# Nystrom attention and a multiplicative feed-forward on one core: transposes moved to VectorE, a recalibrated planner with searched due times, and the 32x32 iteration of two batches in one step

## The chip, the cores and the metric

The kernel runs on one core of one Trainium2 chip. The metric is the device time of one execution, in microseconds; the median of three runs is given. The engines are TensorE (PE), VectorE (DVE), ScalarE (ACT), GpSimd (POOL) and SyncE (SP, which only issues transfers). Each has its own queue and works through it in order; engines meet at semaphores.

## The reference

For each of 8 batches and 8 heads (576 rows, 64 columns), in cut form:

```python
q_lm = q.reshape(B, H, 32, 18, D).mean(axis=3)      # landmarks: means over 18 rows
k_lm = k.reshape(B, H, 32, 18, D).mean(axis=3)
A  = softmax(scale * q    @ k_lm.T)                 # 576 x 32
Bm = softmax(scale * q_lm @ k_lm.T)                 # 32 x 32
C  = softmax(scale * q_lm @ k.T)                    # 32 x 576
Z  = Bm.T / (norm1(Bm) * norminf(Bm) + 1e-6)
for _ in range(6):
    Z = 2 * Z - Z @ Bm @ Z
x = heads_side_by_side(A @ Z @ C @ v)               # 4608 x 512
out = ((x @ w1) * (x @ w2) @ w3) @ w_out            # 4608 x 512
```

## The kernel before

The work is cut into quads, a quad n being four heads of one batch (16 quads, n = 2b + qd), and into batches b (8).

For a quad, two POOL transfers load k and q as fp16 into `nat` (L387). A transposing transfer on SP turns both into `T` (`trans`, L417). POOL sums 18 rows to one (`mean_a`, `mean_b`, L424 to L436), scales the means into `lm` (`mean_c`, L438), and a second transposing transfer on SP makes `lmT` (`lm_trans`, L450). PE computes the scores of C and B into a PSUM pair of their own, `psS` (`s_mm`, L457), and the scores of A (`a_mm`, L533). DVE takes maxima, ACT exponentials, DVE the 32x32 block transposes `ecT` and `aT` (L529, L589); POOL normalises A into `ah` (L582).

For a batch, PE multiplies C with v (`cv_mm`, L640; v is loaded with zeros beside it, so that two heads share 128 rows), DVE and ACT do B's softmax (`b_soft_a` to `b_soft_c`, L669 to L693), and the iteration runs as one PE step and one DVE step five times (`it_mm` L726, `it_out` L736), then Z (L748, L758), W = (Z C v) transposed (L768, L776), and U = W w1 and W w2, 4 x 16 matmuls of 512 columns (L784), which ACT copies to `u` (L798).

The dense part d1 multiplies `u` with `aT`: for a chunk of 288 rows and each of 8 blocks j, four matmuls of 288 columns fill two PSUM banks, one for w1 and one for w2 (`d1_mm`, L854); ACT copies the first out (`d1_a`, L864) and DVE multiplies it with the second into `ab` (`d1_b`, L869). d2 (`d2_mm`, L876) multiplies `ab` with `w34` = w3 @ w_out, eight matmuls of 512 columns for 128 rows; ACT scales it into `osb` and SP stores it in four transfers (L883, L889). `w34` is made in the kernel: `w3` comes in fp32, PE transposes it, ACT and DVE split it into a high and a remaining fp16 part, and 192 matmuls of 512 columns follow (L290 to L350).

The order on all engines is written by a planner (`Plan`, L39). Each piece of work is a task with an engine, an assumed duration, the tasks it needs, slots that it takes from rings of buffers, slots that it frees and a priority. `run` (L86) simulates the engines: at each step it starts the task that can begin first, among near ones that of lowest priority value, and the list that results is the program's order. Priorities are due times: batch b's dense part is due at 66 + 25.5 b (L232 to L243). PSUM is a ring "P" of six banks for everything but `psS`. `wof`, the landing place of w_out, lies in `vbs`, and `ab` is laid over the memory of w34's inputs, so every d1 task waits for the last w34 task (`deps + ["wo7"]`, L908).

Of the kernel before, what the change touches and what calls it, by code (L numbers as in the profile page):

```python
# [20 lines left out]
NC9 = 9  # L21
DM = 512
DF = 1024
HALF = 288
# [3 lines left out]
LOW = -1e30  # L28


class Task:
    def __init__(self, name, eng, dur, fn, deps, acq, rel, prio, mode, lat, move, after):
        self.name, self.eng, self.dur, self.fn = name, eng, dur, fn
        self.deps, self.acq, self.rel = deps, acq, rel
        self.prio, self.mode, self.lat, self.move, self.after = prio, mode, lat, move, after
        self.start = self.ready = None


class Plan:  # L39
# [3 lines left out]
    LAT = {"PE": 0.25, "ACT": 0.08, "DVE": 0.08, "POOL": 0.1, "SP": 0.0}  # L43
    SWITCH = 0.1
# [8 lines left out]
    def add(self, name, eng, dur, fn, deps=(), acq=(), rel=(), prio=0.0, mode=None, lat=None,  # L53
            move=0.0, after=0.0):
        t = Task(name, eng, dur, fn, list(deps), list(acq), list(rel), prio, mode,
                 self.LAT[eng] if lat is None else lat, move, after)
        self.by[name] = t
        self.tasks.append(t)
        return t

    def _slots(self, acq):

        got, when, taken = [], 0.0, {}
        for ring, key, n, uses in acq:
            free = self.rings[ring]
            used = taken.setdefault(ring, set())
            if n == 1:
# [3 lines left out]
                best = min(some, key=lambda i: (free[i], -(free[i ^ 1] is None) if ring == "P" else 0, i))  # L71
                pick = [best]
            else:
# [5 lines left out]
                best = min(some, key=lambda i: max(free[i], free[i + 1]))  # L79
# [5 lines left out]

    def run(self):  # L86
        free = {e: 0.0 for e in self.LAT}
        mode, moved = None, 0.0
        todo = list(self.tasks)
        waiting = {t.name: sum(1 for d in t.deps) for t in todo}  # L90
        after = {}
        for t in todo:
# [3 lines left out]
        for t in todo:  # L96
            if not waiting[t.name]:
                t.ready = 0.0
                avail[t.eng].append(t)
        order = []  # L100
        n = len(todo)
        while len(order) < n:
            best = None
            for e, cand in avail.items():
                opts = []
                for t in cand:
                    found = self._slots(t.acq)
                    if found is None:
                        continue
                    at = max(free[e], t.ready, found[0], t.after)  # L110
                    opts.append((at, t, found[1]))
                if not opts:
                    continue
                first = min(o[0] for o in opts)
                near = [o for o in opts if o[0] <= first + (0.05 if e == "PE" else 0.0)]
                at, t, got = min(near, key=lambda o: (
                    o[1].prio - (0.6 if e == "PE" and o[1].mode == mode else 0.0)))
                if best is None or at < best[0]:
                    best = (at, t, got)
            if best is None:  # L120
                left = [t.name for t in todo if t.start is None]
# [5 lines left out]
            dur = t.dur  # L127
            if e == "PE":
                if t.mode != mode:
                    dur += self.SWITCH  # L130
                mode = t.mode
            free[e] = at + dur
            end = at + dur + t.lat
            if t.move:
                moved = max(moved, at + dur) + t.move
                end = moved + t.lat
            t.end = end
# [5 lines left out]
            for key in t.rel:  # L143
                rec = self.left[key]
                rec[0] -= 1
                rec[1] = max(rec[1], end)
# [3 lines left out]
            for u in after.get(t.name, ()):  # L150
                waiting[u.name] -= 1
                if not waiting[u.name]:
                    u.ready = max(self.by[d].end for d in u.deps)
                    avail[u.eng].append(u)
            order.append(t)
        return order


@with_exitstack
def kernel(  # L160
# [18 lines left out]
    psS = banks[3]  # L179
# [8 lines left out]
    P.ring("P", 6)  # L188
    P.ring("S", 1)
    nats = slots(fixed, 4, [128, 2, GRP, D], FP16, "nat")  # L190
    Ts = slots(fixed, 3, [128, 2 * NC9, 128], FP16, "T")
    lsum = slots(fixed, 1, [128, 2, NC9, D], FP32, "ls")
    lm16 = slots(fixed, 2, [128, 3, 2, D], FP16, "lm")
# [801 lines left out]
```

## Time and profile before

| what | us |
|---|---|
| median of three runs | 351.21 |
| the three runs | 348.2, 351.21, 351.9 |
| span of the profiled execution (first instruction to last) | 343.6 |
| PE busy by records | 277.7 |
| DVE, ACT, POOL busy by records | 201.0, 148.4, 154.2 |

The profiled execution is listed by its span alone; no time of its own beside it is given. A record of a PE instruction ends where the profiler models its result to be complete, so records of neighbours overlap, and the busy time of an engine is the union of its records. In the groups, the figures are busy time and the mean of one instruction, then the idle time of the engine ahead of them and who ended it.

### The profile page before, as it was taken

The numbers are of one execution on the slowest core, as the hardware profiler recorded it, in microseconds if no ns is written. First come the engines' busy times: TensorE is split into PE (matmuls) and PEld (weight loads), VectorE is DVE, ScalarE is ACT, GpSimd is POOL, SyncE is SP. The second block draws the span as 40 slices with busy tenths as digits, with TensorE's granted clock in tenths as the row PEclk, the third lists the DMA queues.
The fourth block names the chain that finished last, engine by engine and source line by source line (L and its number), as shares of the span: only waits on it lengthen the run. The fifth ranks groups of instructions, "written<-read, shape, count | busy, mean of one in ns | idle before, by whom it ended". The sixth has DMA issues, their size and how long they took to land.

```text
span 343.6 us, 10423 instructions
## 1 busy us (share of the span) xinstructions
PE 277.7 (81%) x4288; PEld 152.7 (44%) x4288; DVE 201.0 (58%) x499; ACT 148.4 (43%) x349; POOL 154.2 (45%) x197
## 2 busy tenths in 40 slices
PE   3689888987738878897978899889898887997972
PEld 2244444633523534454535554544455444544531
DVE  7623546461987855684887487755867773432420
ACT  3522332405432344364526555653655255436432
POOL 6498594399783662655485583637011010000000
PEclk9999999999978969999999999999999999999998
DMA  8987989998897886369887997776541210221223
GB/s 214 358 184 152 220 223 207 178 195 177 133 220 82 144 187 129 73 128 192 180 161 169 188 190 144 173 156 138 126 108 32 56 39 3 60 65 32 60 62 93
DMA packets 64175, 48.39 MB, mean 141 GB/s; under 512 B 48256, under 2 KB 48256, under 8 KB 64128
## 3 DMA queue, kind: packets, MB, share of 16 engines
q1 hardware_dynamic: 58368, 36.19, 47.1%
q0 software_dynamic: 5760, 11.54, 20.8%
q8 instruction: 33, 0.54, 0.7%
q14 instruction: 14, 0.11, 0.1%
HBM read 38.80 MB, written 9.44 MB: 140 GB/s over the span
## 4 chain that ended last, share of the span: by engine, by line
PE 44%; DVE 19%; ACT 13%; DMA 11%; issue 5%; SPq 3%; POOL 3%; ACTq 0%; DVEq 0%; POOLq 0%
PE bank L228 44%; DVE ab L872 5%; ACT asb L866 4%; DMA nat<-in_q_dram 4%; ACT u L800 4%; DMA lmT<-lm 3%; DMA vb<-in_moe_w_out_dram 3%; ACT osb L885 2%; DMA vb<-in_v_dram 2%; POOL ls L427 1%; DVE xz L739 1%; DVE xz L722 1%; DVE bm L673 1%; ACT ec L513 1%; SPq L293 1%
## 5 line engine op out<-in xcount | busy, mean ns | idle before, releaser
L228 PE MATMUL bank<-aT,u 128*128 128x288 f16 x512 | 84.0, 291 | 17.2 <-DVE ab L872 8.0
L872 DVE TENSOR_TENSOR ab<-asb,bank 128x288 f16<-128x288 f16 x128 | 55.9, 447 | 56.5 <-ACT asb L866 31.9
L866 ACT CAST asb<-bank 128x288 f16<-128x288 f32 x128 | 49.9, 404 | 72.6 <-PE bank L228 59.9
L228 PE MATMUL bank<-w,ab 128*128 128x512 f16 x288 | 73.7, 382 | 3.5 <-ACT osb L885 1.2
L228 PEld LDWEIGHTS <-u 128*128 128x128 f16 x512 | 47.1, 98 | 48.4 <-issue 28.4
L228 PE MATMUL bank<-wo,w3t 128*128 128x512 f16 x192 | 48.9, 387 | 6.5 <-DVE w3t L331 3.8
L434 POOL TENSOR_TENSOR ls<-ls 128x512 f32<-128x512 f32 (+1 forms) x64 | 46.6, 728 | 4.5
L427 POOL TENSOR_TENSOR ls<-nat 128x1152 f32<-128x1152 f16 x16 | 37.8, 2366 | 20.6 <-DMA nat<-in_q_dram 20.0
L800 ACT CAST u<-bank 128x512 f16<-128x512 f32 x64 | 35.2, 598 | 19.1 <-PE bank L228 12.2
L228 PEld LDWEIGHTS <-ab 128*128 128x128 f16 x288 | 26.9, 98 | 29.0 <-issue 7.0
L885 ACT ACTIVATE osb<-bank 128x512 f32<-128x512 f32 x36 | 21.5, 598 | 30.3 <-PE bank L228 17.1
L582 POOL TENSOR_TENSOR ah<-ea,tiny 128x576 f16<-128x576 f32 x16 | 18.5, 1158 | 29.0 <-DVE tiny L577 21.2
L521 POOL TENSOR_TENSOR tiny<-tiny,maskS 128x4 f32<-128x4 f32 x16 | 3.2, 201 | 61.3 <-ACT ec L513 61.3
L228 PEld LDWEIGHTS <-w3t 128*128 128x128 f16 x192 | 17.8, 98 | 26.9 <-issue 9.7
L228 PE MATMUL bank<-xz 32*32 32x64 f32 (+1 forms) x768 | 20.5, 223 | 11.3 <-DVE xz L722 4.6
L228 PE MATMUL bank<-w,wT 64*32 64x512 f16 x512 | 22.8, 388 | 7.8 <-ACT u L800 2.2
L331 DVE SCALAR_TENSOR_TENSOR w3t<-bank,w3t 128x512 f16<-128x512 f32 x16 | 10.9, 685 | 27.1 <-ACT w3t L324 19.4
L228 PEld LDWEIGHTS bank<-xz 32*32 32x32 f32 x768 | 13.0, 108 | 28.2 <-issue 12.3
L739 DVE SCALAR_TENSOR_TENSOR xz<-xz,bank 128x128 f32<-128x128 f32 x40 | 11.4, 284 | 16.8 <-PE bank L228 16.0
L513 ACT ACTIVATE ec<-bank,tiny 128x320 f32<-128x320 f32 x32 | 16.8, 529 | 9.2 <-DVE tiny L506 8.9
L348 ACT ACTIVATE w<-bank 128x512 f16<-128x512 f32 x8 | 4.8, 596 | 35.0 <-PE bank L228 35.0
L228 PE MATMUL bank<-vb,ecT 128*32 128x128 f32 x576 | 18.0, 273 | 0.1
(75 smaller groups left out, 320.0 us busy)
## 6 DMA issues: line engine op xcount, KB each, us to landing
vb<-in_v_dram SPq DMA_DIRECT2D x64, 144.0 KB, 4.1
out_dram<-osb SPq DMA_DIRECT2D x144, 64.0 KB, 1.7
nat<-in_k_dram POOLq DMA_DIRECT2D x16, 288.0 KB, 5.3
nat<-in_q_dram POOLq DMA_DIRECT2D x16, 288.0 KB, 7.0
w3n<-in_moe_w_dram SPq DMA_DIRECT2D x8, 512.0 KB, 6.9
vb<-in_moe_w_out_dram SPq DMA_DIRECT2D x8, 256.0 KB, 8.6
w<-in_moe_w_dram POOLq DMA_DIRECT2D x8, 256.0 KB, 8.7
T<-nat SPq DMA_TRANSPOSE x16, 5.9
```

What stands on the lines that cost most here:

```text
L228: nc.tensor.matmul(out_, lhsT, rhs, start=start, stop=stop, **({} if pos is None else {"tile_position": pos}))
L331: nc.vector.scalar_tensor_tensor(out=t[:, 1, 512 * h:512 * h + 512], in0=bank(at(f"ptr{j}{h}")), scalar=WSC, in1=t[:, 0, 512 * h:512 * h + ...
L348: nc.scalar.activation(out=w34[:, j, :], in_=bank(at(f"pw{j}")), func=AXF.Copy, scale=1.0 / (WSC * WSC))
L427: nc.gpsimd.tensor_tensor(out=l, in0=nat[:, :, 0:9, :], in1=nat[:, :, 9:18, :], op=ALU.add)
L434: nc.gpsimd.tensor_tensor(out=l[:, :, x:x + m, :], in0=l[:, :, x:x + m, :], in1=l[:, :, y:y + m, :], op=ALU.add)
L513: nc.scalar.activation(out=ecs[at(f"ec{n}")][:, hp, :, :], in_=psS[:, :, 160 * hp:160 * hp + 160], func=AXF.Exp, scale=SCALE, bias=t[:, 2 ...
L582: nc.gpsimd.tensor_tensor(out=ahs[at(f"ah{n}")], in0=eas[at(f"ea{n}")], in1=tinies[at(f"ta{n}")][:, 0:18].unsqueeze(2).to_broadcast([128, ...
L739: nc.vector.scalar_tensor_tensor(out=new.rearrange("p s t x -> p (s t x)"), in0=xz.rearrange("p s t x -> p (s t x)"), scalar=2.0, in1=bank ...
L800: nc.scalar.copy(out=uu[at(f"u{b}{qd}")][:, wi, 512 * half:512 * half + 512], in_=bank(at(f"pU{b}{wi}{half}{qd}")))
L866: nc.scalar.copy(out=asb[at(f"as{b}{j}{ch}")], in_=bank(at(f"pD{b}{j}{ch}0"))[:, 0:HALF])
L872: nc.vector.tensor_mul(abs_[at(f"ab{b // 2}")][:, j, c0:c0 + HALF], asb[at(f"as{b}{j}{ch}")], bank(at(f"pD{b}{j}{ch}1"))[:, 0:HALF])
L885: nc.scalar.activation(out=osb[at(f"os{g}{t}")], in_=bank(at(f"pE{g}{t}")), func=AXF.Copy, scale=2.0 ** -12)
```

## The change

What stays the same: the operations of d2, U, W, w34's 192 matmuls, the split into high and remaining parts, POOL's sums. What changes:

- q, k, the landmarks and `aT` are transposed on DVE as pairs of fp16, taken as one fp32: `T`, `lmT` and `ah` hold pairs side by side, and the scores run as two accumulating matmuls over 32 rows each (e = 0, 1) in place of one over 64. The transposing transfers on SP are gone. B's scores are a nineteenth group of A's, so B's softmax is part of A's; `b_norm` (DVE) writes it to `bm`.
- The scaling of the means moves from POOL to ACT. The swap of maxima is one matmul. v is loaded without zeros, and C runs as 64-row by 32-column tiles.
- w3 is loaded in four transfers of 1 KB rows for each block, transposed on DVE in 32x32 blocks instead of on PE, and w_out lies in `u` and `ab`. `ab` has memory of its own, in four pieces of 384 rows, so d1 doesn't wait for `wo7`; only d2 does.
- The iteration runs for groups of batches: `GROUPS` of one, two, two, two and one.
- d1 has chunks of 192 rows: w1's and w2's part lie in one bank. PSUM is one ring of eight banks; the scores take pairs from it.
- A store is two transfers of 64 partitions instead of four of 32.
- The planner has other costs and latencies, models the two DMA queues, and its due times are two tables, `ANCHOR` (one for each w3 block, quad, batch, dense chunk and group) and `OFF` (one for each kind of task).

The diff, cut to its core:

```diff
-HALF = 288
+CH = 192
+GROUPS = ((0,), (1, 2), (3, 4), (5, 6), (7,))
...
-    LAT = {"PE": 0.25, "ACT": 0.08, "DVE": 0.08, "POOL": 0.1, "SP": 0.0}
-    SWITCH = 0.1
+    LAT = {"PE": 0.23, "ACT": 0.16, "DVE": 0.13, "POOL": 0.1, "SP": 0.0}
+    SELF = {"PE": 0.0, "ACT": 0.14, "DVE": 0.11, "POOL": 0.05, "SP": 0.0}
+    SWITCH = 0.093
+    FIRST, LAND = 1.4, 0.6
...
+ANCHOR = {
+    "z": 0.0, "w0": -55.6, "w1": -74.9, "w2": -57.5, "w3": -88.7, "w4": -90.5, "w5": -59.7, "w6": -54.2,
...
+    "d7": 134.6, "d8": 173.8, "d9": 24.5, "d10": 25.8, "d11": 32.3, "d12": -83.6, "d13": 5.2, "d14": 95.8,
...
-    P.ring("P", 6)
-    P.ring("S", 1)
+    P.ring("P", 8)
...
     def w3_tr(j, h):
-                nc.tensor.transpose(out=ps[:, 128 * i:128 * i + 128],
-                                    in_=w3n[at(f"w3n{j}")][:, 128 * c:128 * c + 128],
-                                    identity=ident[:, :])
+            nc.vector.transpose(
+                out=w3f[at(f"w3f{j}")][:, 4 * h:4 * h + 4].rearrange("p e g i -> p (e g i)"),
+                in_=w3n[at(f"w3n{j}")][:, :, 128 * h:128 * h + 128]
+                .rearrange("p g (e x) -> p e g x", x=32))
...
-    def trans(n):
-            nc.sync.dma_start_transpose(
-                out=Ts[at(f"T{n}")][:, :, :],
-                in_=nats[at(f"nat{n}")].rearrange("p t r d -> p (t r d)"))
+    def trans(n, t):
+            nc.vector.transpose(
+                out=Ts[at(f"T{n}")][:, t].rearrange("p r l e -> p (r l e)").bitcast(FP32),
+                in_=nats[at(f"nat{n}")][:, t].rearrange("p r d -> p (r d)").bitcast(FP32))
...
     def mean_c(n):
+            nc.scalar.activation(out=lm16[at(f"lm{n}")], in_=lsum[at(f"ls{n}")][:, :, 0, :],
+                                 func=AXF.Copy, scale=1.0 / GRP)
...
     def lm_trans(n):
+            nc.vector.transpose(
+                out=lmTs[at(f"lmT{n}")].rearrange("p t l e -> p (t l e)").bitcast(FP32),
+                in_=lm16[at(f"lm{n}")].rearrange("p t d -> p (t d)").bitcast(FP32))
...
     def s_mm(n):
+            for e in range(2):
+                for hh in range(4):
...
+                        mm(ps[o:o + 32, hp, 0:288], lm[r, 1, :, e],
+                           T[r, 0, 9 * t:9 * t + 9, :, e].rearrange("p r l -> p (r l)"),
+                           start=(e == 0), stop=(e == 1), pos=(32 * hh, o))
...
     def a_mm(n):
+            for g in range(GRP + 1):
+                for e in range(2):
+                    for hh in range(4):
+                        r = slice(32 * hh, 32 * hh + 32)
+                        w = lm[r, 1, :, e] if g == GRP else T[r, 1, g, :, e]
+                        mm(ps[r, g, :], w, lm[r, 0, :, e], start=(e == 0), stop=(e == 1),
+                           pos=(32 * hh, 32 * hh))
...
     def a_norm(n):
+                out=ahs[at(f"ah{n}")].rearrange("p g m e -> p g e m"),
...
+    def b_norm(n):
+            nc.vector.tensor_tensor(
+                out=bms[at(f"bm{i}")][:, 0, n - 2 * GROUPS[i][0], :], in0=eas[at(f"ea{n}")][:, GRP, :],
+                in1=tinies[at(f"ta{n}")][:, GRP:GRP + 1].to_broadcast([128, M]), op=ALU.mult)
...
     def cv_mm(b):
+                        mm(ps[o:o + 32, qd, 0:D], ecTs[at(f"ecT{n}")][r, hp, c, :],
+                           vbs[at(f"vb{n}")][r, hp, c, :], start=(c == 0), stop=(c == 8),
+                           pos=(r.start, o))
...
-    def it_mm(b, i):
-            for s in range(2):
+    def it_mm(i, x):
+            for s in range(2 * len(GROUPS[i])):
...
+    def d1_ps(b, j, ch):
+        return bank(at(f"pD{b}{j}{ch}"))[:, 0:2 * CH].rearrange("p (w x) -> p w x", w=2)
...
     def d2_store(i):
+            for x in range(2):
...
+                    in_=o_sb[64 * x:64 * x + 64, :])
...
-                acq = [("P", f"pD{b}{j}{ch}{wi}", 1, 1) for wi in range(2)]
-                add(f"d{b}{j}{ch}", "PE", 0.5, d1_mm(b, j, ch), deps=deps + ["wo7"], acq=acq,
+                add(f"d{b}{j}{ch}", "PE", 0.33, d1_mm(b, j, ch), deps=deps,
+                    acq=[("P", f"pD{b}{j}{ch}", 1, 1)],
```

More of the change, by code (lines that the diff above doesn't have):

```diff
@@ L151, in run @@
                 waiting[u.name] -= 1
+                same = t.eng == u.eng and not t.dma
+                u.ready = max(u.ready, t.free + self.SELF[e] if same else t.end)
                 if not waiting[u.name]:
-                    u.ready = max(self.by[d].end for d in u.deps)
                     avail[u.eng].append(u)
@@ new lines, in quad_tasks @@
+        add(f"lv{n}", "SP", 1.9, load_v(n), acq=[("vb", f"vb{n}", 1, 1)],
+            at=(l, -9.0 + qd), early=-3.0, floor=12.0, dma=("SP", 2.0),
+            kind="lv")
+        loads = [f"lq{n}0", f"lq{n}1"]
+        for t in range(2):
+            add(f"T{n}{t}", "DVE", dve(576), trans(n, t), deps=[loads[t]] + ([f"T{n}0"] if t else []),
+                acq=[] if t else [("T", f"T{n}", 1, 2)], rel=[f"nat{n}"], at=(p, -6.0 + t), kind="T")
+        add(f"ma{n}", "POOL", 2.4, mean_a(n), deps=loads, acq=[("ls", f"ls{n}", 1, 1)],
+            rel=[f"nat{n}"], at=(p, -8.0), kind="mean")
```

806 lines of the change are left out of this document (370 added, 436 removed), and 12 rows, old and new, of tables (ANCHOR, OFF).

## The prediction

> **What bounds the kernel now.** I read the page's busy shares and slices first, then the engine waits of the tensor engine (PE), then the groups by shape, the timeline for the true pace of a matmul, and the DMA queue's waits.
>
> ```profile
> span 343.6 us, 10423 instructions
> PE 277.7 (81%) x4288; PEld 152.7 (44%) x4288; DVE 201.0 (58%) x499; ACT 148.4 (43%) x349; POOL 154.2 (45%) x197
> ...
> PE   3689888987738878897978899889898887997972
> ...
> PE 44%; DVE 19%; ACT 13%; DMA 11%; issue 5%; SPq 3%; POOL 3%; ACTq 0%; DVEq 0%; POOLq 0%
> ```
>
> PE looks full, but less than half of the chain that ends last is PE. The waits of PE say who holds it:
>
> ```profile
> PE bank L228 <- DVE ab L872: 12.6, 23, 1.6
> ...
> PE bank L228 <- ACT u L800: 5.1, 12, 1.0
> PE bank L228 <- DVE xz L722: 4.6, 2, 3.3
> PE bank L228 <- ACT asb L866: 4.5, 15, 0.7
> PE bank L228 <- DVE w3t L331: 3.8, 6, 1.0
> PE bank L228 <- ACT osb L885: 3.5, 7, 0.9
> ```
>
> The first column is us in total. Four of these (L872, L800, L866, L885; 25.7 us) are waits for a PSUM bank to be emptied. The timeline gives the pace behind the records:
>
> ```profile
> 320.81 1.14 PE L228 MATMUL bank<-aT,u 128*128 128x288 f16 x8
> ...
> 326.15 0.65 PE L228 MATMUL bank<-aT,u 128*128 128x288 f16 x4
> ...
> 327.96 1.03 PE L228 MATMUL bank<-w,ab 128*128 128x512 f16 x4
> ...
> 332.22 4.04 PE L228 MATMUL bank<-w,ab 128*128 128x512 f16 x18 [0.69 <-ACT osb L885]
> ```
>
> Four more 288-column matmuls take 1.14 - 0.65 = 0.49 us, 122.5 ns each; fourteen more of 512 take 3.01 us, 215 ns each: 224 more columns in 92.5 ns are 2.4 columns per ns, with 2.5 ns beside them. A record lasts 286 or 379 ns, so a stretch that ends in a wait carries a tail of 0.16 us.
>
> PE's work, at these paces and, for the small kinds, from the start of one group in the timeline to that of the next: d1 512 x 0.1225 = 62.7; d2 288 x 0.215 = 61.9; W3*W_out 192 x 0.215 = 41.3; U 32 x 0.43 = 13.8 (sixteen of 512 columns, eight side by side); C 8 x 2.08 (66.91 to 68.99) = 16.6; the iteration 8 x (0.27 + 5 x 0.36 + 0.26) = 18.6 (72.10 to 72.46); scores 16 x (S 0.28, A 0.32, swap 0.17) = 12.3 (from 46.50 and 63.26); w3 transposes 16 x 0.44 (45.32 to 45.76) = 7.0; W 8 x 0.38 = 3. Together 237 us, 69% of the span. The other 106: idle 343.6 - 277.7 = 66; a clock of 0.84 and 0.83 in 100 to 140 us, 40 x 0.165 = 6.6; the rest, some 33, tails. So the kernel is bound by waits of PE, in a fixed order, and the work itself is a floor far below.
>
> **The change, part by part, on PE.** The w3 transposes leave PE: -7.0. C was 72 passes of 128 columns, four tiles side by side; it becomes 144 of 64 columns, eight side by side, so half of 2.08: -8.3. A was 40 matmuls of 64 columns in 0.32 us and becomes 152 of 32, four side by side: by columns 1.9 times, 0.61 us, by count 3.8 times, 1.22; the row is the same kind of stream of small tiles, so I take columns: 16 x 0.29 = +4.6 (end +14.4). S's sixteen matmuls double in columns (0.15 to 0.30, from the starts at 46.50 and 46.65) and lose four for B: +0.3. The swap becomes one matmul: -1.5. The iteration runs in five groups instead of eight; of a step's 0.36 us, columns are 16 x 64 x 2 / 4 / 2.4 = 0.21, so merging two batches saves a restart of 0.15 in each of 7 steps, three times: -3.2. d1 is 768 matmuls of 192 columns, 80 + 2.5 ns each, 63.4: +0.7. d2, U and w34 stay. Sum -14.4, to 223.
>
> The weights of d1 bear a second look. A weight load's record is 98 ns, longer than the 82.5 ns of the new matmul; if it could not be hidden, 768 x 15.5 = +12 us. At 288 columns the pace is columns alone, which shows it hidden there; I take zero and keep 12. [...]
>
> **The waits.** d1 held two of six banks and now holds one of eight, so three times as many can be under way while ScalarE (ACT) and VectorE (DVE) empty them. Of the 25.7 us I let a third stay: -17. What is late next is DVE's multiply itself. The iteration's waits (L722, L739, L719, L760, L743, L689, L664, L712, L780, L489, L687: 16.8 us) fall with five chains for eight: -6. Both ends are 0 and all of it. The waits for w3 halves (L331 and L324, 5.6) and its second load go by half: -3; the first load at 4.76 us stays. The lmT transfer on PE: -1.4. Tails go with the stops, 33 to 18: -15 (ends 0 and -25). Both dips of the clock come just after PE's thinnest stretch (6.3 of 10 us busy in 90 to 100); a denser PE should not have them: -6.6 (end 0).
>
> **The other engines.** DVE gains, by rows: q/k transposes 32 x 0.77 (L529's 0.835 at 640, less 64 columns at 0.96 per ns) = 24.6; landmark transposes 16 x 0.245 (L691) = 3.9; w3 transposes 16 x 0.70 = 11.2; d1 products 192 x 0.347 against 55.9, +10.7; B's normalisation 16 x 0.225 = 3.6. It loses B's softmax and copy, 16.4, half of aT's transposes, 4.8, and some 10 in iteration, maxima and constants. Net +23 on records that sum to 222. Two L872 back to back take 0.82 for 2 x 0.45, so 0.08 of each record overlaps: occupied 182 now, 201 after (some 548 instructions). In 287 us that is 70%, hidden beside PE's 78% as long as the order alternates. ACT: 192 x 0.32 for 49.9, +11.7, and the mean's scaling +5: 148 to 163, hidden. GpSimd (POOL): loses 16.8 (mean's scaling), 8.5 (memsets), 3.2 and four issues; its normalisation now writes every second fp16: between its row 1.16 and the 2.37 of L427, up to 16 x 1.2 = 19 on an engine at 43%; I take zero.
>
> SP loses 32 DMA transposes and half of the 144 stores, and gains 24 w3 issues at about 0.45 us, 11 us, in the first stage, where v's loads wait behind them; hidden, since before it needed the time for transposes:
>
> ```profile
> SPq L419 <- PE bank L228: 30.9, 12, 4.3
> SPq L419 <- DMA nat<-in_q_dram: 23.7, 6, 17.1
> SPq L452 <- POOL lm L445: 19.2, 5, 7.3
> ```
>
> These waits do not vanish: the transposes that stood in SP's queue now stand in DVE's, with the d1 products and the iteration behind them, and PE's banks behind those. If the order places them late enough they cost nothing, which I assume.
>
> DVE operations with two SBUF inputs vary while others do not: L722 has a mean of 683 ns and 213 at best, L673 618 and 224, L743 440 and 224, L689 426 and 225, mean excess 320; L739, with one input in PSUM, keeps 284.
>
> ```profile
> L722 DVE TENSOR_TENSOR xz<-bm,tiny 128x64 f32<-128x64 f32 x8 | 5.5, 683 | 0.0
> L739 DVE SCALAR_TENSOR_TENSOR xz<-xz,bank 128x128 f32<-128x128 f32 x40 | 11.4, 284 | 16.8 <-PE bank L228 16.0
> L529 DVE STREAM_TRANSPOSE ecT<-ec 128x640 f32<-128x640 f32 x16 | 13.4, 835 | 1.6 <-ACT ec L513 1.4
> ```
>
> The change adds 32 such (16 w3 remainders, whose source was PSUM; 16 of B) and removes 22: 10 x 0.32 = 3 us of DVE, hidden. [...]
>
> **Sum.** 343.6 - 14.4 - 17 - 6 - 3 - 1.4 - 15 - 6.6 = 280.2. The profiled execution has no time of its own beside its span; the median of 351.2 lies 7.6 above it, and I add that: 287.8, say 287.
>
> **Rivals.** (a) More than that: all bank and iteration waits go and tails fall by 25: 280.2 - 8.7 - 10.8 - 10 = 250.7, so 258 at best, about 268 in the middle. For it: banks are eight, and PE's records already fill 9.69 of the 10 us from 20 to 30; against: DVE at 75 to 80%. (b) DVE becomes the bound: 201 + 13 (42 two-input operations by 0.32), at the 69% that PE gets now from a fixed order, 310, with 7.6 it is 318. For it: DVE is 19% of the chain already. (c) Only the work goes, and the waits move to new places: 343.6 - 14.4 + 7.6 = 337. (d) Weight loads and the small matmuls of A cost their upper ends, 12 + 9.8: 309. [...] (e) Slower: DVE waits in order for loads, as SP did. All of 30.9 + 23.7 + 19.2 = 74 us put on DVE and PE: 287 + 74 = 361. It decides from 64 us on, 1.3 us for each of the 48 moved transposes. For it: a place in a fixed queue cannot move when a load is late; against: L419's 30.9 are waits for a free buffer, and DMA without 48256 small packets should land earlier than now (q 7.0 us).
>
> **Chances.** Forecast (274 to 302) 0.44; (a) 0.16; (b) 0.13; (c) 0.08; (d) 0.05; (e) 0.12; no change 0.02. Faster by over 1% is 0.86, within 1% 0.02 (about what a measurement here can tell), slower 0.12. The range must leave out 0.2: (e) and no change, and 0.06 of the ends of (a) and (c): 262 to 338.
>
> **What would show it.** Right: records of d1 at 192 columns with starts 82 ns apart; A near 0.6 us; PE's waits on L872's successor below 9 us; a clock of 1.00 after the first 15 us; q/k transposes near 0.77 us with no wait for a DMA ahead of them. Wrong: DVE over 80% busy with PE waiting on it, transposes that wait for loads, or PE starts of d1 98 ns or more apart. The forecast falls if the searched order leaves PE's idle time near 66 us.

## The result and the profile after

| | before | after |
|---|---|---|
| median of four runs, same chip | 351.55 us | 440.12 us |
| ratio, 95% interval | 1 | 1.2508 (1.2391 to 1.2624) |
| span of the profiled execution | 343.6 us | 433.7 us (its time: 435.43) |
| granted TensorE clock, mean | 0.978 | 0.869 |
| PE busy; idle (span less busy) | 277.7; 65.9 | 295.0; 138.7 |
| pairs of weight load and matmul on PE | 4288 | 6728 |

A pair is one weight load and the matmul that follows it: two instructions of PE. Some executions of each kernel are slower than its others; ratios leave these out, and the profiled executions of the runs b1 and s4 below are such ones, so that of them only the place and kind of the waits is relied on.

The change costs 88.6 us where 64 were forecast to be gained. The page of the changed kernel, in the parts shown of before:

```profile
span 433.7 us, 15201 instructions
PE 295.0 (68%) x6728; PEld 188.8 (44%) x6728; DVE 218.3 (50%) x540; ACT 157.6 (36%) x421; POOL 124.8 (29%) x137
...
PEclk9999999986559975579879886579979998999999
...
q8 instruction: 52, 0.85, 0.8%
```

No engine is fuller than it was: DVE is at 50%. The clock row has three holes. The last line (packets, MB) is the queue that brings instructions; before, it had 33 packets:

```profile
q8 instruction: 33, 0.54, 0.7%
```

At 128 pairs to a packet (worked out below), 52 packets are 6656 of PE's 6728 pairs, and 33 are 4224 of 4288: the queue carries PE's instructions. The waits of PE (us in total, times, longest) name two things ahead of all others:

```profile
PE bank L277 <- issue: 57.5, 28, 5.5
PE bank L277 <- ACT w3t L349: 40.4, 1, 40.4
PE bank L277 <- DVE ab L860: 10.0, 18, 1.6
PE bank L277 <- ACT u L781: 9.0, 16, 1.4
PE bank L277 <- ACT asb L854: 6.5, 16, 0.8
PE bank L277 <- ACT osb L874: 2.7, 5, 0.7
```

Before, the same two stood at:

```profile
PE bank L317 <- DMA w3n<-in_moe_w_dram: 6.8, 2, 4.8
...
PE bank L228 <- issue: 0.3, 1, 0.3
```

`issue` is time in which PE waited for nothing that the profile shows. The second line of the changed kernel is one wait: its first matmul comes at 40.4 us. These two grew by 57.2 and 33.6, 90.8 together, and the idle time by only 72.8, so the other waits fell, by 18.0.

**Where `issue` stands.** PE's timeline from 100 us (start, us, then the group; the bracket is the idle time before it):

```profile
101.30 1.39 PE L277 MATMUL bank<-vb,ecT 64*32 64x64 f32 x72
103.73 1.23 PE L277 MATMUL bank<-vb,ecT 64*32 64x64 f32 x69 [1.05 <-issue]
...
105.48 0.38 PE L277 MATMUL bank<-lmT,T 32*32 32x32 f16 x24
107.46 1.15 PE L277 MATMUL bank<-lmT,T 32*32 32x32 f16 x120 [1.60 <-issue]
108.43 0.25 PE L277 MATMUL bank<-lmT 32*32 32x32 f16 x8
114.21 0.36 PE L277 MATMUL bank<-xz 32*32 32x64 f32 x5 [5.52 <-issue]
```

C (`vb,ecT`), A (`lmT,T`) and the iteration (`xz`), all in tiny matmuls, follow each other, and PE stops in the middle of a task whose operands are there. The number of pairs between two stops is 128 or a multiple of it: 125 to 128 in 18 of the 27 intervals, 253 to 255, 382 to 384, 512 and 768 in the others. PE's semaphore instructions make up the rest: with them counted, the instructions started from one stop to any other agree with 256 for each packet landed between, within one, at all 28 stops. In the same stretch the trace's DMA records have packets of 16384 bytes on the queue of kind "instruction", at 101.06, 104.78, 111.68 and 115.30 us: 3.6 or 3.7 us apart, and once 6.9, where the longest stop is. From 100 to 120 us the clock is 0.55, from 160 to 180 it is 0.50.

**Where the first 40 us go.** SP's queue, then DVE's:

```profile
0.74 2.76 SPq L315 DMA_DIRECT2D u<-in_moe_w_out_dram  x4
3.54 18.68 SPq L315 DMA_DIRECT2D ab<-in_moe_w_out_dram  x4
22.26 17.04 SPq L322 DMA_DIRECT2D w3n<-in_moe_w_dram  x12
```

```profile
37.73 0.69 DVE L335 SCALAR_TENSOR_TENSOR wo<-ab,wo 128x512 f16<-128x512 f32 x1 [2.13 <-ACT wo L330]
...
39.03 0.67 DVE L341 STREAM_TRANSPOSE w3f<-w3n 128x512 f32<-128x512 f32 x1
```

Before, the eight had been issued by 5.7 us:

```profile
1.19 4.49 SPq L293 DMA_DIRECT2D vb<-in_moe_w_out_dram  x8
```

Now eight transfers of w_out hold SP until 22.3 us, w3 stands behind them, and on DVE and ACT the first w3 block stands behind all eight blocks of w_out. The new source of w_out, which the lines of the diff above do not include, is a view whose first dimension has four entries: `moe_w_out.rearrange("(a e c) f -> e a c f", a=4, e=8)[c]` in place of 128 rows. From 4 to 22 us, when w_out alone stands on SP's DMA queue, this queue fills 15.8% of the time of the 16 engines, and in 17.0 of the 18 us no more than four of its packets are under way at once (never more than six); before, with w_out and w3 on it, it filled 51.8% from 0 to 6 us, with up to 19 packets under way. Why a view of this form brings so few packets at a time is not shown. The last of the eight blocks is taken up by DVE at 37.7 us. Two experiments below (e2 and b2) change only the view.

**What came as forecast.** Groups of the changed kernel (busy us, mean ns of one, idle time before them):

```profile
L441 DVE STREAM_TRANSPOSE T<-nat 128x576 f32<-128x576 f32 x32 | 24.1, 757 | 0.0
L860 DVE TENSOR_TENSOR ab<-asb,bank 128x192 f16<-128x192 f16 x192 | 60.5, 349 | 60.2 <-ACT asb L854 32.6 <-PE bank L277 21.6 <-ACT u L781 3.9
L854 ACT CAST asb<-bank 128x192 f16<-128x192 f32 x192 | 54.9, 327 | 36.9 <-PE bank L277 18.5 <-DVE ab L860 14.8 <-DVE xz L719 0.8
L566 POOL TENSOR_TENSOR ah<-ea,tiny 128x576 f16<-128x576 f32 x16 | 18.7, 1174 | 92.1 <-DVE tiny L561 58.4 <-ACT osb L874 18.3 <-ACT u L781 13.8
```

Transposes of q and k take 757 ns and wait for no load (0.0), a product 349 (0.347 forecast), an ACT copy 327 (0.32), POOL's normalisation 1174, no more than before. d1 and A on PE:

```profile
53.63 1.32 PE L277 MATMUL bank<-lmT,T 32*32 32x32 f16 x144
54.78 0.24 PE L277 MATMUL bank<-lmT 32*32 32x32 f16 x8
54.84 0.47 PE L277 MATMUL bank<-T,lmT 32*32 32x288 f16 x16
...
410.27 2.15 PE L277 MATMUL bank<-aT,u 128*128 128x192 f16 x24 [1.09 <-DVE ab L860]
412.85 0.82 PE L277 MATMUL bank<-aT,u 128*128 128x192 f16 x8 [0.43 <-ACT asb L854]
```

Sixteen more d1 matmuls take 2.15 - 0.82 = 1.33 us, 83 ns each: the weight loads (12 us in the prediction's upper end) are hidden. A, where nothing holds it, needs 54.84 - 53.63 = 1.21 us for 152 matmuls, 8 ns each: by count, not by columns. C, where nothing holds it, starts its 144 passes within 1.5 us (the last at 345.37), at a clock of 1.00:

```profile
343.88 1.66 PE L277 MATMUL bank<-vb,ecT 64*32 64x64 f32 x140
```

The forecast was half of 2.08, 1.04.

### The profile page after: what moved, and what is told of

Same layout as the page of the kernel before. It is cut to its first block, busy times and chain, and to the rows that moved or that the text cites. A ratio compares the mean times of both kernels' runs of the same rounds, so it can differ in the third digit from the quotient of the medians.

```text
span 433.7 us, 15201 instructions
## 1 busy us (share of the span) xinstructions
PE 295.0 (68%) x6728; PEld 188.8 (44%) x6728; DVE 218.3 (50%) x540; ACT 157.6 (36%) x421; POOL 124.8 (29%) x137
## 4 chain that ended last, share of the span: by engine, by line
PE 57%; issue 16%; ACT 10%; DVE 8%; DMA 4%; SPq 4%; ACTq 0%; DVEq 0%
PE bank L277 57%; DMA ab<-in_moe_w_out_dram 4%; SPq L315 4%; ACT asb L854 4%; ACT u L781 4%; DVE ab L860 3%; ACT osb L874 1%; DVE T L441 1%; DVE w3f L341 1%; DVE w3t L356 0%; DVE xz L719 0%; DVE bm L576 0%; DVE wT L763 0%; ACT w L375 0%; DVE aT L583 0%
## 5 line engine op out<-in xcount | busy, mean ns | idle before, releaser
L860 DVE TENSOR_TENSOR ab<-asb,bank 128x192 f16<-128x192 f16 x192 | 60.5, 349 | 60.2 <-ACT asb L854 32.6
L277 PE MATMUL bank<-aT,u 128*128 128x192 f16 x768 | 79.4, 253 | 13.8 <-ACT asb L854 6.0
L277 PEld LDWEIGHTS <-u 128*128 128x128 f16 x768 | 66.6, 100 | 30.7 <-issue 21.8
L277 PE MATMUL bank<-wo,w3t 128*128 128x512 f16 x192 | 47.7, 403 | 45.2 <-ACT w3t L349 40.4
L854 ACT CAST asb<-bank 128x192 f16<-128x192 f32 x192 | 54.9, 327 | 36.9 <-PE bank L277 18.5
L277 PEld LDWEIGHTS <-w3t 128*128 128x128 f16 x192 | 19.1, 103 | 69.6 <-ACT w3t L349 40.4
L277 PEld LDWEIGHTS <-ab 128*128 128x128 f16 x288 | 27.9, 99 | 41.5 <-issue 13.4
L566 POOL TENSOR_TENSOR ah<-ea,tiny 128x576 f16<-128x576 f32 x16 | 18.7, 1174 | 92.1 <-DVE tiny L561 58.4
L277 PE MATMUL bank<-lmT,T 32*32 32x32 f16 x2304 | 23.5, 181 | 17.3 <-issue 17.1
L511 ACT ACTIVATE ec<-bank,tiny 128x288 f32<-128x288 f32 x32 | 15.9, 503 | 39.2 <-DVE tiny L503 34.1
L277 PEld LDWEIGHTS <-T 32*32 32x32 f16 x2304 | 21.1, 91 | 20.6 <-issue 19.9
L277 PE MATMUL bank<-vb,ecT 64*32 64x64 f32 x1152 | 18.0, 255 | 13.0 <-issue 13.0
L441 DVE STREAM_TRANSPOSE T<-nat 128x576 f32<-128x576 f32 x32 | 24.1, 757 | 0.0
L719 DVE SCALAR_TENSOR_TENSOR xz<-xz,bank 128x256 f32<-128x256 f32 (+1 forms) x25 | 9.1, 362 | 27.1 <-PE bank L277 26.1
## 6 DMA issues: line engine op xcount, KB each, us to landing
w<-in_moe_w_dram POOLq DMA_DIRECT2D x4, 512.0 KB, 12.6
```

The costliest lines, as they stand in the source:

```text
L277: nc.tensor.matmul(out_, lhsT, rhs, start=start, stop=stop, **({} if pos is None else {"tile_position": pos}))
L441: nc.vector.transpose(out=Ts[at(f"T{n}")][:, t].rearrange("p r l e -> p (r l e)").bitcast(FP32), in_=nats[at(f"nat{n}")][:, t].rearrange(" ...
L511: nc.scalar.activation(out=ecs[at(f"ec{n}")][:, hp, :], in_=banks[at(f"pS{n}") // 2][:, hp, 0:288], func=AXF.Exp, scale=SCALE, bias=t[:, 2 ...
L566: nc.gpsimd.tensor_tensor(out=ahs[at(f"ah{n}")].rearrange("p g m e -> p g e m"), in0=eas[at(f"ea{n}")][:, 0:GRP, :].rearrange("p (g e) m - ...
L719: nc.vector.scalar_tensor_tensor(out=new[:, 0:ns].rearrange("p s t x -> p (s t x)"), in0=xz[:, 0:ns].rearrange("p s t x -> p (s t x)"), sc ...
L854: nc.scalar.copy(out=asb[at(f"as{b}{j}{ch}")], in_=d1_ps(b, j, ch)[:, 0, :])
```

## The experiments

Theory: PE's instructions are supplied at a limited rate, and tiny matmuls use them up faster; beside it, the head of the kernel is late through w_out's transfers and the fixed queues behind them. Rivals: the searched order or the grouping of the iteration makes the waits; tiny matmuls are slow in themselves; the bank and clock steps of the prediction hold and are hidden by something else. `issue` and "first matmul" are read from the profiled execution of each kernel; every ratio is to the kernel before on the same chip.

| run | us | ratio (95%) | pairs | issue, us | first matmul, us |
|---|---|---|---|---|---|
| e1_wide_a | 383.89 | 1.1066 (1.1001 to 1.1130) | 4680 | 17.1 | 40.7 |
| e2_wout_32rows | 424.85 | 1.2249 (1.2156 to 1.2343) | 6728 | 56.9 | 28.0 |
| e3_wide_a_wout | 369.66 | 1.0660 (1.0627 to 1.0693) | 4680 | 16.5 | 26.6 |
| b1_narrow_a (from before) | 398.43 | 1.1458 (1.1383 to 1.1534) | 5952 | 34.0 | as before |
| b2_wout_4d (from before) | 365.88 | 1.0455 (1.0379 to 1.0531) | 4288 | - | waits 15.7 on w3 |
| b3_d1_one_bank (from before) | 351.70 | 1.0020 (0.9973 to 1.0066) | - | - | as before |
| g1_groups_of_one | 439.89 | 1.2552 (1.2454 to 1.2650) | - | 52.5 | 40.4 |
| f1_wide_a_head | 371.87 | 1.0599 (1.0516 to 1.0682) | 4680 | 17.8 | 29.0 |
| s1_spread | 394.56 | 1.1207 (1.1088 to 1.1326) | 6728 | 20.0 | 27.6 |
| s2_spread_plain | 405.85 | 1.1575 (1.1470 to 1.1681) | 6728 | 31.5 | 17.1 |
| s3_plain | 419.27 | 1.1911 (1.1787 to 1.2035) | 6728 | 45.5 | 17.7 |
| f2_wide_a_front | 368.31 | 1.0564 (1.0461 to 1.0668) | 4680 | 17.0 | 12.4 |
| f3_wide_a_front_c | 368.38 | 1.0559 (1.0458 to 1.0659) | 4680 | 10.2 | 12.4 |
| s4_spread_front | 393.75 | 1.1246 (1.1115 to 1.1376) | 6728 | 21.3 | 11.8 |
| f4_wide_a_front_few_c | 335.96 | 0.9672 (0.9579 to 0.9765) | 3784 | 2.3 | 12.6 |

**e1, e2, e3: the two causes apart and together.** e1 swaps weights and moving operand in A (A comes out transposed), so that 24 wide matmuls do the columns of 152; e2 loads each block of w_out as four transfers of 32 rows; e3 does both.

```diff
-            for g in range(GRP + 1):
+            for g0, g1 in ((0, 16), (16, 18), (18, 19)):
...
-                        mm(ps[r, g, :], w, lm[r, 0, :, e], start=(e == 0), stop=(e == 1),
+                        mm(ps[r, g0:g1, :].rearrange("p g m -> p (g m)"), lm[r, 0, :, e], x,
...
-            nc.sync.dma_start(out=wof[at(f"wf{c}")],
-                              in_=moe_w_out.rearrange("(a e c) f -> e a c f", a=4, e=8)[c])
+            for a in range(4):
+                nc.sync.dma_start(out=wof[at(f"wf{c}")][32 * a:32 * a + 32, :],
+                                  in_=moe_w_out[256 * a + 32 * c:256 * a + 32 * c + 32, :])
```

> The changed kernel with A's scores as 24 matmuls of 512, 64 and 32 columns per quad instead of 152 of 32 columns; the landmarks are the stationary side, so A comes out transposed and the output is not the reference's; columns per quad, order and all other engines' work are the same. Theory (PE runs out of instructions: its idle time put down to issue is 57.5 us, and the gaps come after exactly 256 or 512 instructions): PE has 4680 matmuls instead of 6728, the issue idle falls under 20 us, the mean clock rises from 0.87 to above 0.93, and the time falls from 440 to 375 to 400 us. Rival (the fixed order and its waits between engines cost the time): as many columns, same order, so 430 to 440 us.

> The changed kernel with each w_out block loaded by four transfers of 32 rows instead of one transfer whose source has an outer dimension of 4; same bytes to the same places, same order. Theory (each of those transfers runs on few DMA engines, so eight of them hold SP for 22 us and the first matmul waits until 40.4 us): first matmul at 15 to 22 us, time 415 to 422 us. Rival (the head is covered, because nothing before d2 needs w34): 435 to 440 us.

> Both edits of the two runs above; A transposed, so not the reference's output. Theory: both gains add, 355 to 380 us. Rival (waits of the order): 425 us or more.

PE's first waits in e1, then in e2:

```profile
PE bank L277 <- ACT w3t L349: 40.7, 1, 40.7
PE bank L277 <- issue: 17.1, 9, 3.6
```

```profile
PE bank L277 <- issue: 56.9, 27, 5.1
PE bank L277 <- ACT w3t L350: 28.0, 1, 28.0
```

Each edit moves its own wait and leaves the other where it was. e1 and e3 fell within their ranges of time (e1's clock, 0.920, stayed short of the 0.93 forecast). e2 missed: first matmul at 28.0 us instead of 15 to 22, and 424.85 us instead of 415 to 422; its 32 transfers of w_out still held SP until 20.2 us. From e2 to e3, on one chip, 2048 pairs less bring 424.85 - 369.66 = 55.2 us, 27 ns a pair, though A does the same columns. Some 10 us of this is A's own pace (0.58 us a quad in e3 by the starts of its groups, 1.21 in the changed kernel); `issue` fell by 40.4. From e1 to e3 the head brings 14.2 us.

**b1, b2: the same two put into the kernel before.** b1 cuts each matmul of A into pieces of 16 columns (same result); b2 gives w_out's loads the new form (its rows come permuted).

```diff
-                    if c < 4:
-                        mm(ps[hc, 0, 64 * c:64 * c + 64], T[:, c, hc], kb, pos=pos)
...
+                        for y in (0, 16):
+                            mm(ps[hc, e, x + y:x + y + 16], T[:, c, hc], kb[:, i, y:y + 16], pos=pos)
```

> The kernel before, with each of A's 64-column matmuls cut into four of 16 columns with the same weights: 160 instead of 40 per quad, the same columns, the same result, the same order. Theory (instruction supply): 1920 more pairs, gaps on PE put down to issue after 256 or 512 instructions, time 375 to 400 us. Rival (only the pace of small matmuls, 7.3 ns each as in before's A, 120 x 16 x 7.3 ns = 14 us if none is hidden): at most 366 us and no issue gaps.

> The kernel before with w_out loaded by transfers of the changed kernel's form (source with an outer dimension of 4, so its rows land permuted and the output is not the reference's); all else the same. Theory (such a transfer runs on few DMA engines): the eight of them hold SP for about 20 us instead of 4.5, the first w34 chain of eight is complete only near 35 us, and the time rises by 10 to 22 us, to 358 to 372. Rival (slow landing in the changed kernel came from the other loads beside it): at most 352 us.

b1 is 398.43 - 347.81 = 50.6 us slower for 1664 pairs more, 30 ns a pair, without a searched table, a group or a DVE transpose. (The edit makes 144 matmuls a quad, not the 160 of its expectation.) At the 8 ns of a free burst, A's own pace would be an estimated 13 us of it; that alone, the rival's case, would stay under 366 us. b2 is 365.88 - 350.74 = 15.1 us slower. Each cause acts by itself. PE's longest waits in b1, then in b2:

```profile
PE bank L228 <- issue: 34.0, 13, 8.2
```

```profile
PE bank L318 <- DMA w3n<-in_moe_w_dram: 15.7, 2, 11.5
```

**b3, g1: two steps of the forecast.** b3 gives the kernel before d1 in chunks of 192 rows, w1's and w2's part in one bank; g1 runs the iteration of the changed kernel batch by batch.

```diff
-HALF = 288
+HALF = 192
...
-                    mm(ps[:, 0:HALF], uu[at(f"u{b}{qd}")][:, wi, 128 * j:128 * j + 128],
+                    mm(ps[:, HALF * wi:HALF * wi + HALF], uu[at(f"u{b}{qd}")][:, wi, 128 * j:128 * j + 128],
```

```diff
-GROUPS = ((0,), (1, 2), (3, 4), (5, 6), (7,))
+GROUPS = tuple((b,) for b in range(8))
```

> The kernel before with d1 in chunks of 192 rows, both products in one PSUM bank, due times spread over three chunks; nothing else of the change. The prediction's step (three times as many d1 steps under way, two thirds of 25.7 us of bank waits gone): 330 to 341 us. Rival (the waits are those of DVE and ACT, which work more on short chunks, and only move): 345 to 355 us.

> The changed kernel with its iteration in eight groups of one batch; the pairs' due times are used for both members; the planner orders anew. The prediction's step (fewer chains, fewer waits): slower by 5 to 10 us than the changed kernel, 445 to 450. Rival (a pair waits for the scores of two batches, while PE's instruction supply is the same): 430 to 438 us. If neither matters: 440.

The bank waits of b3 are these:

```profile
PE bank L228 <- DVE ab L872: 11.4, 29, 0.9
PE bank L228 <- ACT u L800: 6.3, 13, 1.2
...
PE bank L228 <- ACT osb L885: 5.4, 11, 1.0
```

With ACT's `asb` (2.8) they sum to 25.9 us; before they were 25.7. One bank instead of two makes them shorter (0.9 us at most on `ab`, 1.6 before) and more frequent (29, 23 before), and the time stays within 0.7%. b3 keeps the ring of six banks, so it has twice as many d1 steps under way, not the eight of the changed kernel. Without grouping (g1) the changed kernel takes 439.89 us, with it 440.12: no difference that can be seen. PE's waits for the iteration's `xz`, `wT`, `zb` and `tiny` are 11.9 us in g1 and 3.8 with grouping, but `issue` is 52.5 and 57.5.

**m1: the supply by itself.** No attention: streams of matmuls with 32x32 weights on four row positions, and nothing on the DMA queues but PE's instructions until the output is stored.

> No attention at all: 768 matmuls of 256 columns, 768 of 128, 768 of 64, 1536 of 32 and 1536 of 16, each with its own weight load, on four 32x32 tiles in turn, nothing else on the chip until the output is stored (zeros and constants). Theory (PE's instructions arrive in blocks of 256, one block in 3.3 to 3.6 us): once the stock is used up, a pair takes 26 to 28 ns whatever its columns, so 40 us for 1536 pairs of 16 or of 32 and 20 us for 768 of 64 or 128. Rival (the pace of the array alone): 27 ns at 256 columns, 13 at 128, 7 at 64, 3.5 to 7 at 32 and 16, so 5 to 11 us for 1536 pairs.

```profile
71.09 1.22 PE L60 MATMUL p<-x,w 32*32 32x32 f16 x128 [2.04 <-issue]
75.09 1.22 PE L60 MATMUL p<-x,w 32*32 32x32 f16 x128 [2.78 <-issue]
78.54 1.22 PE L60 MATMUL p<-x,w 32*32 32x32 f16 x128 [2.24 <-issue]
```

Groups of exactly 128 pairs run in 1.22 us each, and PE stands idle for the rest of 3.4 to 4.0 us. Per pair it is 31.1 ns at 256 columns, where PE does not stop, and then 27.2 at 128, 28.4 at 64, 28.7 at 32, 28.4 at 16: no matter how narrow. 16384 bytes for 256 instructions are 64 bytes each; in the narrow streams one packet came about every 3.7 us. PE's waits for `issue` come to 78.7 of the 183.3 us.

**f1, s1, s2, s3: the head, bursts, the searched tables.** f1 is e3 with w_out's transfers in turn on SP and ACT and the first w3 block first on SP. s1 keeps all matmuls, has f1's head, and plans A's 152 and C's 80 as five pieces each, 1.1 us apart. s2 is the same (1.0 us apart) with plain due times, a batch every 25.5 us; s3 is s2 with A and C whole.

```diff
-        add(f"A{n}", "PE", 0.6, a_mm(n), deps=both, acq=[("P", f"pA{n}", 2, 1)],
+        for x in range(5):
+            add(f"A{n}{x}", "PE", 0.13, a_mm(n, x), deps=[f"A{n}{x - 1}"] if x else both,
+                acq=[] if x else [("P", f"pA{n}", 2, 1)], lat=None if x == 4 else 1.1,
```

> The changed kernel with A as 24 wide matmuls a quad (A comes out transposed), every block of w_out as four transfers of 32 rows issued in turn by SP and ACT, and the first two... the first block of w3 put at the head of SP's queue. Theory (two causes: small matmuls that outrun PE's instruction supply, and a late w_out/w3): the first matmul of w34 comes at 8 to 14 us instead of 26.6, and 10 to 16 us go from the 369.7 us of the run with wide A and 32-row transfers: 352 to 360 us. Rival (something later sets the end, such as loads of q and k or the searched order): the head is early, and the time stays within 4 us of 369.7.

> The changed kernel, all its matmuls kept (A and C with the same small matmuls and results), the same early head as in the run before; A's 152 matmuls of a quad and C's 80 of a batch are planned as five pieces each, 1.1 us apart, so that w34, d1 or output matmuls can stand between the pieces. Theory (bursts cost, since the supply is about 28.5 ns for a load and matmul pair while 6728 pairs in all need only 192 us of it): issue time falls from 57.5 us to below 25, and the time to 360 to 380 us. Rival (every small matmul costs 28 ns wherever it stands): the issue time stays over 45 us and only the head is gained: 400 to 420 us.

> As the run before (all matmuls kept, pieces 1.0 us apart), with due times by a plain rule (a batch every 25.5 us) in place of the searched tables. Theory that the searched order in itself matters little: within 3 % of the run before. Rival that the search put the bursts and loads where they hurt: over 3 % faster; that it was worth having: over 3 % slower.

> As the run before, with A and C whole again (one burst of 152 and one of 80 each). Theory of bursts: 20 to 50 us slower than with the pieces, and issue time over 40 us. Rival (total of instructions): within 8 us of it.

f1 missed: the load was early, the first matmul was not (29.0 us). DVE and ACT still had the eight blocks of w_out ahead of w3. s1 took 37 us of `issue` away and the time went from e2's 424.85 to 394.56 at nearly the same head (27.6 and 28.0 us; by the ratios some 36 us less), short of the forecast 360 to 380. From s3 to s2, on one chip, pieces bring 419.27 - 405.85 = 13.4 us and 14.0 us of `issue`; theory (20 to 50) and rival (within 8) both missed. So places between large matmuls help, but not all of the pairs find cover. The plain tables are 2.9% slower than the searched ones (s2 to s1), with an earlier head; the search did not make the loss: with plain tables and A and C whole (s3) the kernel stays 19% slower than the one before.

**m2: the rule.** Groups of 0, 16, 32, 64 and 128 small matmuls, each followed by three of 128x128 by 512 columns.

> No attention: only groups of small matmuls (32x32 weights, 32 columns) with three matmuls of 128x128 by 512 columns after each group, 0, 16, 32, 64 or 128 small ones a group. Theory (supply of 128 pairs per 3.66 us, 28.6 ns a pair, with a reserve of at most 256 pairs, and execution that covers it): a group takes the longer of execution (three times 215 ns, and 9.5 ns for each small one) and 28.6 ns for each of its pairs: 0.65, 0.80, 1.00 (supply) or 0.95, 1.92 and 3.75 us a group. Rival (only long bursts starve): up to 64 small ones a group cost execution alone, 1.25 us at 64.

DVE copies a result after 160, 60, 50, 40 and 20 groups:

```profile
108.13 0.19 DVE L68 COPY o<-y 128x32 f32<-128x32 f32 x1 [106.16 <-PE y L67]
164.39 0.19 DVE L68 COPY o<-p 128x32 f32<-128x32 f32 x1 [56.07 <-PE p L64]
217.09 0.19 DVE L68 COPY o<-p 128x32 f32<-128x32 f32 x1 [52.51 <-PE p L64]
292.50 0.19 DVE L68 COPY o<-p 128x32 f32<-128x32 f32 x1 [75.22 <-PE p L64]
365.82 0.19 DVE L68 COPY o<-p 128x32 f32<-128x32 f32 x1 [73.13 <-PE p L64]
```

A group takes 0.66, 0.94, 1.05, 1.89 and 3.67 us. Up to 32 small ones that is about execution (0.94 at 16, where 0.80 was forecast); at 64 it is 1.885 / 67 = 28.1 ns a pair where execution alone, by the starts in its timeline (0.59 us for 64 small, 0.75 for three large), would be 1.34; at 128 it is 28.0 ns. The rival (64 cost execution alone) falls. Here large matmuls covered small ones as long as the work of a group came to 28 ns or more for each of its pairs (1.05 us for 35 pairs, 30 ns, at 32 small ones); at 64 it came to 1.34 us for 67, 20 ns, and what was missing to 28 was idle time. The theory's reserve is measured in the changed kernel: counted from its stops, where none are left, the packets landed never held more than 524 instructions, 262 pairs, that PE had not started.

**f2, f3, s4: what is left with wide A.** f2 puts w3's first block, with its transposes and halves, ahead on all three queues; f3 adds C in five pieces; s4 is s1 with f2's front.

```diff
+    j = w3a.name[3:]
+    go = [w3a.name, "wf0", "wf1", f"tr{j}0", f"wh{j}0", f"wl{j}0", f"tr{j}1", f"wh{j}1", f"wl{j}1"]
+    order = [P.by[x] for x in go] + [t for t in order if t.name not in go]
```

> The changed kernel with wide A (A comes out transposed) and the four 32-row transfers of each w_out block on SP (two), ACT and POOL; the first block of w3, its two transposes and its four halves of weights now stand at the head of the SP, ACT and DVE queues, behind two blocks of w_out only. In the run with the early load alone the first matmul stayed at 29.0 us, since DVE and ACT took all eight blocks of w_out first. Theory (the order of the queues holds w34 up): first matmul at 9 to 16 us and 8 to 16 us less than the 371.9 us of that run, so 355 to 364. Rival (the work that w34 delays fits in elsewhere, the end is set by another chain): first matmul as early, time within 4 us of 371.9.

> As the run before, with C's 80 matmuls of a batch (160 passes, its operands being fp32) planned as five pieces 1.0 us apart. Theory of bursts: the issue time that is left with wide A (17.8 us) falls to below 8 us, and the time by 8 to 14 us, to 342 to 354 us, about the kernel before. Rival (C's gaps are covered): issue falls, the time stays within 4 us.

> The changed kernel with all its matmuls and its results, A and C in five pieces each 1.1 us apart (394.6 us in the earlier run), and the queues' front as in the first run of this call. Theory: 10 to 20 us less than 394.6, so 374 to 385 us, and still slower than the kernel before, since 5376 small matmuls of A and C wait on supply wherever large ones do not cover them. Rival: under 355 us, small matmuls cost nothing once spread and started in time.

None gained what the theory said: f2 stays within 4 us of f1, its rival's case, and s4 within 1 us of s1. PE's timeline at the head of f2 shows why an early first matmul brings so little:

```profile
12.39 4.72 PE L277 MATMUL bank<-wo,w3t 128*128 128x512 f16 x10 [12.39 <-ACT wo L331]
18.07 1.89 PE L277 MATMUL bank<-wo,w3t 128*128 128x512 f16 x8 [0.95 <-DVE wo L336]
25.32 1.03 PE L277 MATMUL bank<-wo,w3t 128*128 128x512 f16 x2 [5.36 <-ACT w3t L350]
27.59 6.84 PE L277 MATMUL bank<-wo,w3t 128*128 128x512 f16 x22 [1.24 <-DVE w3t L357]
```

Eighteen of 192 matmuls came early (3.9 us of work at 215 ns); the next ones wait for another w3 block until 25.3 us, and e3's first matmul came at 26.6. In f3 `issue` fell from 17.0 to 10.2 us and the waits for DVE's `ab` and ACT's `asb` rose from 9.9 and 6.7 to 12.8 and 9.5: the rival expected there held. PE's idle time (span less busy) is 88.1 us in f2 and 88.3 in f3. Pieces do not lower the number of pairs; here they only moved the wait.

**f4: most of C left out.** f2 with two of C's nine chunks.

```diff
-            for c in range(NC9):
+            for c in (0, 8):
```

> The run with wide A and the early front (368.3 us), with seven of C's nine chunks left out: 16 of 72 matmuls of a batch and the row sums stay, so 896 fewer passes in all. Theory of bursts (what is left of issue time and of the lowered clock comes from C): issue falls from 17.0 to below 6 us, the clock rises from 0.906 to over 0.95, and the time falls by 15 to 25 us, more than the some 8 us of PE work left out (8 batches by 1.0 us): 343 to 353 us. Rival (the head and the searched order set the end): the time falls by 8 us or less, to 360 us or more.

Its page and its waits for `issue`:

```profile
span 333.9 us, 9356 instructions
PE 258.4 (77%) x3784; PEld 155.7 (47%) x3784; DVE 221.2 (66%) x540; ACT 157.8 (47%) x421; POOL 130.0 (39%) x145
```

```profile
PE bank L277 <- issue: 2.3, 4, 0.9
```

896 pairs less bring 368.31 - 335.96 = 32.4 us (31.2 by the ratios), more than the theory's 15 to 25, some 35 ns each and over three times their own work (1.5 us for 144 pairs where nothing holds C: 9.3 us); the clock rises from 0.906 to 0.958. It is faster than the kernel before, but leaves out most of C.

## Why the prediction was wrong

- **The small matmuls of A** ("the row is the same kind of stream of small tiles, so I take columns") are the step that failed most. Their own pace is the upper end, by count: 1.21 us a quad, not 0.61, some 14 us more than before in all. Rival (d) had this price, and no more. The far larger part was put at nothing: the sum has no term for the supply of instructions. 152 pairs take 152 x 28 ns = 4.3 us to be supplied, of which a burst with little beside it pays most. Before had 40 x 16 = 640 pairs in A, after has 2432: at the 27 ns a pair of e2 and e3, which hold the slower pace too, 1792 pairs are an estimated 48 us. A row that bore on this was there (10423 instructions, 33 packets of the instruction queue), but `issue` was 0.3 us: this said "enough until now", not "never". Within bursts the trace has 8 ns a matmul, and streams of small matmuls have 28 ns a pair on the average (m1).
- **C** ("half of 2.08: -8.3") failed the same way. Where nothing holds it C takes 1.5 us a batch, not 1.04, and 72 passes became 144: 576 pairs more in eight batches, at f4's 35 ns an estimated +20 us.
- **SP's issues and loads** ("hidden, since before it needed the time for transposes") failed. The sum had no term at all for the new source of w_out. It costs 15.1 us by itself in the kernel before (b2), and taking it out of the changed kernel with wide A gains 14.2 (e1 to e3). What is late next was not asked either: in the first 40 us PE has 19.2 us of busy time even in f2, and 28.1 before. No run shows that this costs time: from f1 to f2 it rose from 10.9 to 19.2, and the time fell by 1.2 us by the ratios.
- **Bank waits** ("I let a third stay: -17") failed: 28.2 us after (10.0 + 9.0 + 6.5 + 2.7), 25.7 before; b3, where nothing else changed, 25.9 and no gain. (From two of six banks to one of eight is three steps to eight, 2.7 times as many, not three.) One bank instead of two changed when PE waits, not how long in all; that ACT and DVE, which empty the banks, set this is likely, but no run changes their pace.
- **All waits together.** f4 shows that the gains forecast here did not merely hide under the two new causes: with `issue` down to 2.3 us, PE's idle time is 333.9 - 258.4 = 75.5 us. Less `issue` and the first wait (12.6) it is 60.6; before, less 0.3 and the waits for w3 (6.8), it was 58.8. The prediction had named this sign: it falls if PE's idle time stays near 66 us.
- **The iteration** (-3.2 and -6) is unproved as a gain. Its waits on DVE did fall, from 16.8 us before to 3.8 (`xz`, `wT`, `zb` and `tiny`), 8.1 of it by the grouping (g1); without the grouping the time is the same.
- **The clock** (-6.6) went the other way, 0.978 to 0.869, and is lowest in stretches with `issue` (0.55 and 0.50). The prediction had taken the dips to follow a thin PE; there are now more such stretches. Thinness alone is not the rule: in the first 10 us of before PE has 4.3 us of work, less than in the stretch that the prediction calls thinnest, and in the first 40 us of the changed kernel it has none, both at a clock of 1.00.
- **Tails** (-15) cannot be told apart from the rest; the -14.4 of work and the w3 step (-3) cannot either, beside A and C.
- **Right**: durations on DVE, ACT and POOL, DVE hidden (50%, so rival (b) is not the cause; of its operations with two SBUF inputs the w3 remainders have a mean of 942 ns and 628 at best, B's normalisations 431 and 181, but the eight of w_out keep 687 to 693, so not all of them vary), weight loads hidden, q and k transposes that wait for no load. Rival (e) named the mechanism, work in a fixed queue behind a late load, but put it on q and k; it struck w_out at the head. Its 361 us and the range's 338 are both below the result, since no case had the supply.

The three parts that the runs price add up, as a rough estimate, to 48 (A) + 20 (C) + 15 (w_out) = 83 us, against 88.6 measured; nothing of the forecast gain of 64 is seen beside them. What stays open: how much of f4's 35 ns a pair, beyond 28, is the lowered clock, why a packet takes 3.7 us to come, and what the change is worth with C in its old 72 passes, which was not tried.

## What to carry to other kernels

Count instructions, not columns, wherever matmuls are narrower than what 28 ns of work would be (the supply in m1 and m2): sum the pairs of each burst and of the large work beside it, and where the average comes below 28 ns, the difference is idle time, and the clock was lower there (down to 0.50 in m1, m2 and the changed kernel). A wait that the profile calls `issue` and that returns after multiples of a fixed number of instructions points to that limit. And when a load's source view is changed, look at its first dimension (15.1 us in b2), at what the load's queue is held for, and at everything that stands behind that load in each in-order queue.

## What the runs showed of the hardware

- PE's instructions came in packets of 16384 bytes, 128 pairs, one about every 3.7 us in a stream of small matmuls, whatever their width (m1: 27.2 to 28.7 ns a pair from 16 to 128 columns), with nothing else on the DMA queues.
- Mixed with large matmuls, small ones came free of supply up to 32 for every three large ones, and at 64 and 128 the average was 28.1 and 28.0 ns a pair (m2).
- With the supply short, the clock fell: in m1 to 0.50 from 60 us on; in m2 to 0.91 with 64 small matmuls a group, and to 0.50 from 300 us on with 128, where three matmuls of 512 columns took 1.46 us instead of 0.82.
- Loads of 128 rows whose source view begins with a dimension of four cost 15.1 us in the kernel before (b2); in the changed kernel, from 4 to 22 us, their queue filled 15.8% of the time of the 16 DMA engines.
